# Gated linear attention followed by a maxout feed-forward block: packing transfers issued ahead of loads, output steps moved behind the next group's last unit, weight rounding split in two halves

## The chip, the cores and the metric

One core of a Trainium2 chip runs the whole program. The metric is device time in microseconds of one execution; lower is better. The kernel before and the changed kernel compute the same function on the same inputs.

## The reference

The first block is a linear attention with a gated state, for 4 batches of 8 heads, 768 positions, head size 48. The second is a feed-forward block with three input weights and an elementwise maximum.

```python
f = 1 / (1 + exp(-f_logit))
for t in range(768):                       # per batch and head
    state = f[t][:, None] * state + outer(k[t], v[t])
    y[t]  = q[t] @ state
x = y as (3072 tokens, 384)                # 8 heads side by side
h = maximum(maximum(x @ w1, x @ w2), x @ w3)   # 384 -> 768
out = h @ w_out                            # 768 -> 384
```

The weights arrive as 8-byte words; the kernel rounds them to 4-byte floats itself, with bit operations.

## The kernel before

**Units.** The sequence is cut into chunks of 64 positions. A unit is one chunk of two batches with all heads; there are 24 units, and unit u holds chunk u // 2 of batch pair u % 2. Four units make a group of 512 tokens, so there are 6 groups. For a unit, `sigmoids` and `products` make the gates, their running products (a scan on VectorE, L255), the transposed k and q (through TensorE for units 0 to 7, by VectorE transposes at L232 from unit 8 on) and q times the products; `quotients` makes the reciprocals (L274) and `kh` (GpSimd, L275) in two halves. `keys` transposes `kh` back on TensorE (L288), `pairs` makes the scores (L301) and masks them (L304), `values` multiplies them with v and updates the state (L318 to L335). `finish` adds the part from the state (L348), copies the result from PSUM to `xT` with ScalarE (L357), copies the fourth heads' part to `last` (L354), and **packs** it: six small transfers from `last` into the free rows of `xT` (L362). With them the group's `xT` is a dense 384 x 512 operand.

**Feed-forward block.** `ffn(g, xT)` is a generator of 22 steps: 18 products with a slice of w1, w2 or w3 (L373, 6 TensorE instructions a step) whose results are evacuated by ScalarE (L377) or VectorE (L379), and 4 output steps (L388, 12 TensorE instructions a step), each with a ScalarE copy (L391) and two stores (L395). `fill(n)` runs n steps of it between the parts of the next group's units. Before the next group's `ffn` is made, `fill(99)` empties the old one. Two PSUM tiles take the results of steps in turn.

**Weights.** They come in 15 pieces. `load_weight` (L196) starts a piece's transfer into one of 4 raw buffers. `round_weight` rounds one: VectorE L208, ScalarE L211, GpSimd add L212, VectorE L213, ScalarE L217, VectorE L218, which writes the weight tile; then it starts the load of the piece four further on. Pieces 0 to 2 are rounded after unit 1, pieces 3 to 14 within the steps of group 0, each ahead of its use.

**Order.** The program's order is the order of each engine's instructions; nothing is reordered. Transfers are started by SyncE (SP), one after the other, except k and q of unit 0, which ScalarE starts. A transfer at the head of SP's list that has to wait holds everything behind it. `load(u)` for units up to 7 is 6 transfers (L145) and `load_v` 2; from unit 8 on, `load(u)` of an even unit fetches f, k and q for two units in 24 transfers (L158). In the main loop an even unit u begins with `load(u + 2)` and `load_v(u + 2)`, and only then come `fill`, `keys(u)` and `finish(u - 1, xT)`. In the opening loop over units 0 to 3 `load(u + 4)` and `load_v(u + 4)` follow `values(u)`, ahead of the `finish` of that unit.

Of the kernel before, what the change touches and what calls it, by code (L numbers as in the profile page):

```python
# [9 lines left out]
FP32 = mybir.dt.float32  # L10
I32 = mybir.dt.int32
U32 = mybir.dt.uint32
AF = mybir.ActivationFunctionType
# [31 lines left out]
DP = 64  # L45
# [7 lines left out]
def kernel(  # L53
# [12 lines left out]
    nc = tc.nc  # L66
# [3 lines left out]
    UT = 2 * C  # L70
# [18 lines left out]
    def fast():  # L89
        ctx = ExitStack()  # L90
        with ctx:
# [71 lines left out]
            def load_v(u):  # L163
                load_tokens(v_tiles[u % NLD], v, u)
# [32 lines left out]

            def round_weight(n):
                if n in raw:
                    dst = pieces[n][0]  # L200
                    a, w = dst.shape[1:]
                    N = a * w
                    words = raw.pop(n)[:, 0:2 * N].rearrange("p (n two) -> p n two", two=2)
                    lo, hi = words[:, :, 0], words[:, :, 1]


                    top = work.tile([128, 768], U32, name="top_bits")[:, 0:N]
                    nc.vector.tensor_scalar(top, hi, 3, 0x3FFFFFF8, op0=ALU.logical_shift_left, op1=ALU.bitwise_and)  # L208

                    rest = work.tile([128, 768], U32, name="rest_bits")[:, 0:N]  # L210
                    nc.scalar.activation(rest, lo, AF.Copy, scale=2.0 ** -29)  # L211
                    nc.gpsimd.tensor_tensor(top, top, rest, op=ALU.add)  # L212
                    nc.vector.scalar_tensor_tensor(top, hi, 0xC0000000, top, op0=ALU.bitwise_and, op1=ALU.bitwise_or)  # L213


                    size = work.tile([128, 768], FP32, name="size")[:, 0:N]
                    nc.scalar.activation(size, hi.bitcast(FP32), AF.Square)  # L217
                    nc.vector.scalar_tensor_tensor(dst, size.rearrange("p (a c) -> p a c", a=a), HI_MIN ** 2,  # L218
                                                   top.bitcast(FP32).rearrange("p (a c) -> p a c", a=a),
                                                   op0=ALU.is_ge, op1=ALU.mult)  # L220
                load_weight(n + RAW)

# [116 lines left out]

            def finish(u, xT):  # L340
                d = ready.pop(u)
# [17 lines left out]
                for par in range(2):  # L359
                    for i in range(NK):  # L360
                        p0 = par * DP
                        nc.sync.dma_start(out=xT[p0 + D:p0 + DP, i, t0:t0 + UT],  # L362
                                          in_=last[p0 + i * TAIL:p0 + (i + 1) * TAIL, :])


            def ffn(g, xT):
                hm = work.tile([128, NJ, TOK], FP32, name="hm", bufs=1)
                for j in range(NJ):
                    top = None
                    for i in range(3):  # L370
# [11 lines left out]
                        if g == 0 and (step < 6 or step % 2 == 0):  # L382
                            round_weight(3 + step if step < 6 else 6 + step // 2)
                        yield
# [12 lines left out]

            pending = iter(())

            def fill(n):  # L400
                for _ in range(n):
                    next(pending, None)

# [3 lines left out]


            with tc.manual_schedule():
                for u in range(GRP):  # L410
                    load(u, nc.scalar if u == 0 else nc.sync)
                    load_v(u)
                for n in range(RAW):
# [4 lines left out]
                for u in range(GRP):  # L418
                    keys(u)
                    if u > 1:  # L420
                        finish(u - 1, xT)
                    pairs(u)
                    if u + 2 < GRP:
                        gates(u + 2)
                    values(u)
                    load(u + GRP)
                    load_v(u + GRP)
                    if u == 0:
                        finish(u, xT)
                    if u == 1:  # L430
                        for n in range(3):
                            round_weight(n)

                nc.tensor.transpose(ps_tr.tile([128, 128], FP32, name="tr"), ident, ident)
                finish(GRP - 1, xT)
                pending = ffn(0, xT)
                fill(1)
# [6 lines left out]
                for u in range(GRP, NU):  # L444
                    n = u + 1
                    if BY_ROWS <= u + 2 < NU and u % 2 == 0:
                        load(u + 2)
                    if GRP <= u + 2 < NU and u + 2 >= 2 * GRP:
                        load_v(u + 2)
                    fill(2 if u % 2 and u < NU - GRP else 1)  # L450
                    keys(u)
                    if u > GRP:
                        finish(u - 1, xT)
                    if u % GRP == 0:
                        if u > GRP:
                            fill(99)
                            pending = ffn(u // GRP - 1, xT)
                        xT = new_xT()
                    pairs(u)
                    if n < NU:  # L460
                        sigmoids(n)
# [8 lines left out]
                    if n < NU:  # L470
                        quotients(n, 1)
                        if n in (5, 7):
                            pad_blocks(n // 2 % 2)
                    fill(1)
                fill(1)
                finish(NU - 1, xT)
                fill(99)
                pending = ffn(NU // GRP - 1, xT)
                fill(99)

# [233 lines left out]
```

## Time and profile before

| | us |
|---|---|
| median of 3 runs | 628.8 (626.64 to 629.12) |
| the profiled execution | 628.61 |
| its span in the trace | 626.9 |
| TensorE busy (matmuls) | 484.0 (77% of the span) |
| VectorE busy | 261.3 (42%) |
| ScalarE busy | 127.6 (20%) |
| GpSimd busy | 100.8 (16%) |

The profiled execution took 1.7 us more than its span. Busy time of TensorE includes stretches at the lower of its two clock levels: the granted clock is given as a share of full speed (2.4 GHz), and half is the lower level. The chain that ended last is TensorE for 66% of the span and SP's list of transfers for 12%.

### The profile page before, as it was taken

What the parts mean: (1) busy time and instruction counts of PE and PEld (TensorE: products, weight loads), DVE (VectorE), ACT (ScalarE), POOL (GpSimd) and SP (SyncE); (2) the same over time, 40 slices, a digit from 0 to 9 for tenths busy, and PEclk for the clock granted to TensorE, in tenths of its full rate; (3) what the DMA queues carried; (4) which work ended last, traced back from release to release, by engine and by line L of the source; (5) the groups of instructions that cost most, each with busy time, mean ns of one, the idle gap of its engine ahead of it and who ended that gap; (6) DMA issues with size and microseconds to landing.
All of it is one profiled execution on the core that took longest, in us unless ns stands there. A gap on an engine that the chain in (4) does not pass through costs nothing.

```text
span 626.9 us, 10135 instructions
## 1 busy us (share of the span) xinstructions
PE 484.0 (77%) x4067; PEld 259.5 (41%) x4067; DVE 261.3 (42%) x321; ACT 127.6 (20%) x297; POOL 100.8 (16%) x139
## 2 busy tenths in 40 slices
PE   5830168597991799990999990999981999999995
PEld 3630035154451355560455550455550444554452
DVE  6840055746634256542356532366431466101110
ACT  3431043233221022211022220022220022120000
POOL 4410032444232010110011010011110011000000
PEclk9765597887996799996899995899995999999998
DMA  9756355535026106026015026015035000010001
GB/s 141 167 107 139 66 101 109 126 90 71 4 56 89 29 10 85 18 46 96 16 21 76 17 56 87 14 26 75 13 64 80 13 4 5 17 42 0 0 14 44
DMA packets 166761, 34.99 MB, mean 56 GB/s; under 512 B 155952, under 2 KB 163632, under 8 KB 166704
## 3 DMA queue, kind: packets, MB, share of 16 engines
q1 hardware_dynamic: 164592, 33.85, 31.5%
q10 hardware_dynamic: 2112, 0.39, 0.4%
q8 instruction: 34, 0.56, 0.4%
q14 instruction: 23, 0.19, 0.1%
HBM read 28.31 MB, written 4.72 MB: 53 GB/s over the span
## 4 chain that ended last, share of the span: by engine, by line
PE 66%; SPq 12%; DVE 9%; issue 4%; POOL 3%; DMA 2%; ACT 2%; DVEq 0%; POOLq 0%; ACTq 0%
PE p L373 43%; PE p L388 13%; SPq L158 5%; DVE inv L274 4%; SPq L145 3%; POOL top_bits L212 2%; PE y L348 2%; SPq L362 2%; PE y L318 2%; PE tr L288 2%; PE a L301 2%; DMA xT<-last 1%; PE y L327 1%; DVE top_bits L213 1%; DVE prod L255 1%
## 5 line engine op out<-in xcount | busy, mean ns | idle before, releaser
L373 PE MATMUL p<-xT,w_in 128*128 128x512 f32 x648 | 304.4, 624 | 95.5 <-DMA xT<-last 87.9
L373 PEld LDWEIGHTS p<-xT,w_in 128*128 128x128 f32 x648 | 125.7, 200 | 244.0 <-issue 234.2
L388 PE MATMUL p<-w_out,hm 128*128 128x384 f32 x288 | 95.5, 488 | 1.5 <-DVE hm L379 1.5
L379 DVE TENSOR_TENSOR top<-p,top 128x512 f32<-128x512 f32 x36 | 24.5, 681 | 164.6 <-PE p L373 164.6
L274 DVE RECIPROCAL inv<-prod 128x256 f32<-128x256 f32 x48 | 82.5, 1734 | 0.3
L377 ACT COPY top<-p 128x512 f32<-128x512 f32 x36 | 21.1, 586 | 280.1 <-PE p L373 280.1
L388 PEld LDWEIGHTS p<-w_out,hm 128*128 128x128 f32 x288 | 54.2, 190 | 40.3 <-issue 2.9
L268 POOL TENSOR_TENSOR qh<-qt,prod 128x512 f32<-128x512 f32 x24 | 28.3, 1178 | 206.7 <-DVE qt L232 130.1
L275 POOL TENSOR_TENSOR kh<-kt,inv 128x256 f32<-128x256 f32 x48 | 36.2, 754 | 157.2 <-DVE inv L274 157.2
L379 DVE TENSOR_TENSOR hm<-p,top 128x512 f32<-128x512 f32 x36 | 24.3, 675 | 35.3 <-PE p L373 35.1
L304 DVE TENSOR_TENSOR at<-a,mask 128x512 f32<-128x512 f32 x24 | 16.5, 687 | 51.8 <-PE a L301 51.8
L213 DVE SCALAR_TENSOR_TENSOR top_bits<-raw,top_bits 128x768 uint32<-128x768 uint32 (+1 forms) x15 | 12.0, 800 | 61.2 <-POOL top_bits L212 61.2
L255 DVE TENSOR_TENSOR_SCAN prod<-gate,floor 128x520 f32<-128x520 f32 x24 | 29.7, 1238 | 7.8 <-issue 4.5
L391 ACT COPY o<-p 128x384 f32<-128x384 f32 x24 | 11.5, 479 | 104.7 <-PE p L388 96.6
L212 POOL TENSOR_TENSOR top_bits<-top_bits,rest_bits 128x768 uint32<-128x768 uint32 (+1 forms) x15 | 22.2, 1483 | 62.7 <-ACT rest_bits L211 43.0
L288 PE MATMUL tr<-ident,kh 128*128 128x128 f32 x88 | 16.3, 317 | 17.7 <-POOL kh L275 17.7
L318 PE MATMUL y<-at,v_ld 64*64 64x64 f32 x768 | 18.0, 236 | 9.8 <-issue 8.8
L290 ACT COPY ks<-tr 128x512 f32<-128x512 f32 x22 | 12.9, 585 | 60.2 <-PE tr L288 60.2
L318 PEld LDWEIGHTS y<-at,v_ld 64*64 64x64 f32 x768 | 14.6, 144 | 25.0 <-issue 23.6
L288 PEld LDWEIGHTS tr<-ident,kh 128*128 128x128 f32 x88 | 12.2, 161 | 27.4 <-POOL kh L275 19.9
L357 ACT COPY xT<-y 64x192 f32<-64x192 f32 (+1 forms) x72 | 22.7, 316 | 1.3
L354 ACT COPY last<-y 64x64 f32<-64x64 f32 (+1 forms) x72 | 15.0, 209 | 23.8 <-DMA xT<-last 12.4
(56 smaller groups left out, 275.6 us busy)
## 6 DMA issues: line engine op xcount, KB each, us to landing
v_ld<-in_v_dram SPq DMA_DIRECT2D x48, 96.0 KB, 2.9
out_dram<-o SPq DMA_DIRECT2D x48, 96.0 KB, 2.2
raw<-in_moe_w_dram SPq DMA_DIRECT2D x12, 288.0 KB, 4.8
xT<-last SPq DMA_DIRECT2D x144, 8.0 KB, 1.8
raw<-in_moe_w_out_dram SPq DMA_DIRECT2D x3, 768.0 KB, 4.4
f_ld<-in_f_logit_dram SPq DMA_DIRECT2D x32, 64.0 KB, 2.5
k_ld<-in_k_dram SPq DMA_DIRECT2D x32, 64.0 KB, 2.5
q_ld<-in_q_dram SPq DMA_DIRECT2D x32, 64.0 KB, 2.5
```

The lines of the kernel that those rows point to most:

```text
L158: nc.sync.dma_start(out=blocks[nm][u // 2 % 2][p0:p0 + 32, n, :, 0:w], in_=src[:, par::2, t0 + n * 32:t0 + (n + 1) * 32, e0:e0 + w].rearrange(
L212: nc.gpsimd.tensor_tensor(top, top, rest, op=ALU.add)
L255: nc.vector.tensor_tensor_scan(scan.rearrange("p x t -> p (x t)"), gate.rearrange("p x t -> p (x t)"), floor.rearrange("p x t -> p (x t)") ...
L268: nc.gpsimd.tensor_tensor(qh, qt, prod, op=ALU.mult)
L274: nc.vector.reciprocal(d["inv"][:, a], d["prod"][:, a])
L275: nc.gpsimd.tensor_tensor(d["kh"][:, :, a, :], d["kt"][:, a], d["inv"][:, a], op=ALU.mult)
L288: nc.tensor.transpose(tr_s[:, hp, :], kh[:, hp].rearrange("p a t -> p (a t)"), ident)
L318: nc.tensor.matmul(y[o:o + DP, a, hp * C:(hp + 1) * C], lhsT=v_ld[s, 2 * hp + par, :], rhs=d["at"][s, par, hp, :], start=(hp == 0), stop=F ...
L357: nc.scalar.copy(xT[o, :, t0 + a * C:t0 + (a + 1) * C], y[i, a, 0:NK * C].rearrange("p (h t) -> p h t", h=NK))
L373: nc.tensor.matmul(p, lhsT=w_in[i][:, kt, j * 128:(j + 1) * 128], rhs=xT[:, kt, :], start=(kt == 0), stop=(kt == NK - 1))
L379: nc.vector.tensor_tensor(hm[:, j, :] if i == 2 else top, p, top, op=ALU.max)
L388: nc.tensor.matmul(p[:, 0:DM], lhsT=hm[:, j, i * UT:(i + 1) * UT], rhs=w_out[:, j, :], start=(j == 0), stop=(j == NJ - 1))
```

## The change

1. In the main loop `load(u + 2)` and `load_v(u + 2)` move from the head of unit u to behind `pairs(u)`, that is, behind the packing of unit u - 1.
2. `pending` becomes a list of generators. A group's `ffn` is appended instead of being started after `fill(99)`, so the rest of the old one runs first. From unit 4 to 8 one `fill(1)` less per unit is done, from then on 22 steps per group as before. At the border of two groups (u = 8, 12, 16, 20) one output step stands before `keys(u)` and two stand between `pairs(u)` and `values(u)`.
3. In the opening, the packing of units 0 to 2 is started by ScalarE, that of unit 3 half by SP and half by ScalarE. `load` and `load_v` of unit u + 4 stand behind the `finish` or the rounding of unit u, those of unit 7 behind the packing of unit 3. v of two units is loaded after f, k and q of both.
4. `round_weight(n)` becomes `round_begin(n)` (L208, L211, L212, L217) and `round_end(n)` (L213, L218, next load). A step that needed `round_weight(n)` runs `round_end(n)` and then `round_begin(n + 1)`. Pieces 0 to 2 are begun after unit 1 and ended after unit 2's `values`. `top_bits` and `size` get three buffers.

```diff
+            def round_begin(n):
                 if n in raw:
...
                     nc.vector.tensor_scalar(top, hi, 3, 0x3FFFFFF8, op0=ALU.logical_shift_left, op1=ALU.bitwise_and)
...
                     nc.scalar.activation(rest, lo, AF.Copy, scale=2.0 ** -29)
                     nc.gpsimd.tensor_tensor(top, top, rest, op=ALU.add)
+                    size = work.tile([128, 768], FP32, name="size", bufs=3)[:, 0:N]
+                    nc.scalar.activation(size, hi.bitcast(FP32), AF.Square)
+                    halfway[n] = (top, hi, size)
+
+            def round_end(n):
+                if n in raw:
...
+                    top, hi, size = halfway.pop(n)
                     nc.vector.scalar_tensor_tensor(top, hi, 0xC0000000, top, op0=ALU.bitwise_and, op1=ALU.bitwise_or)
...
+                    del raw[n]
                 load_weight(n + RAW)
...
-            def finish(u, xT):
+            def finish(u, xT, queues=(nc.sync, nc.sync)):
...
-                        nc.sync.dma_start(out=xT[p0 + D:p0 + DP, i, t0:t0 + UT],
+                        queues[par].dma_start(out=xT[p0 + D:p0 + DP, i, t0:t0 + UT],
...
-                            round_weight(3 + step if step < 6 else 6 + step // 2)
+                            n = 3 + step if step < 6 else 6 + step // 2
+                            round_end(n)
+                            round_begin(n + 1)
...
-            pending = iter(())
+            pending = []
...
-                for _ in range(n):
-                    next(pending, None)
+                while n and pending:
+                    try:
+                        next(pending[0])
+                        n -= 1
+                    except StopIteration:
+                        pending.pop(0)
...
-                    load_v(u)
+                    if u % 2:
+                        load_v(u - 1)
+                        load_v(u)
...
-                        finish(u - 1, xT)
+                        finish(u - 1, xT, (nc.scalar, nc.scalar))
...
-                    load(u + GRP)
-                    load_v(u + GRP)
                     if u == 0:
-                        finish(u, xT)
+                        finish(u, xT, (nc.scalar, nc.scalar))
                     if u == 1:
                         for n in range(3):
-                            round_weight(n)
+                            round_begin(n)
+                    if u == 2:
+                        for n in range(3):
+                            round_end(n)
+                        round_begin(3)
+                    if u < GRP - 1:
+                        load(u + GRP)
+                        load_v(u + GRP)
...
-                finish(GRP - 1, xT)
-                pending = ffn(0, xT)
+                finish(GRP - 1, xT, (nc.sync, nc.scalar))
+                load(2 * GRP - 1)
+                load_v(2 * GRP - 1)
+                pending.append(ffn(0, xT))
...
                 for u in range(GRP, NU):
                     n = u + 1
-                    if BY_ROWS <= u + 2 < NU and u % 2 == 0:
-                        load(u + 2)
-                    if GRP <= u + 2 < NU and u + 2 >= 2 * GRP:
-                        load_v(u + 2)
-                    fill(2 if u % 2 and u < NU - GRP else 1)
+                    fill(2 if u % 2 and u > 2 * GRP else 1)
                     keys(u)
                     if u > GRP:
                         finish(u - 1, xT)
                     if u % GRP == 0:
                         if u > GRP:
-                            fill(99)
-                            pending = ffn(u // GRP - 1, xT)
+                            pending.append(ffn(u // GRP - 1, xT))
                         xT = new_xT()
                     pairs(u)
+                    if BY_ROWS <= u + 2 < NU:
+                        if u % 2 == 0:
+                            load(u + 2)
+                        load_v(u + 2)
...
-                    fill(1)
+                    if u >= 2 * GRP:
+                        fill(1)
                 fill(1)
                 finish(NU - 1, xT)
-                fill(99)
-                pending = ffn(NU // GRP - 1, xT)
+                pending.append(ffn(NU // GRP - 1, xT))
                 fill(99)
```

## Rows read from the trace of the kernel before

**Rows 1.** The page's DMA issues: transfers, KB each, median us from issue to landing.

```profile
xT<-last SPq DMA_DIRECT2D x144, 8.0 KB, 1.8
...
q_ld<-in_q_dram SPq DMA_DIRECT2D x32, 64.0 KB, 2.5
```

**Rows 2.** Waits of TensorE, whole span: total us, times, longest.

```profile
PE p L373 <- DMA xT<-last: 87.9, 5, 26.9
PE tr L288 <- POOL kh L275: 17.7, 4, 6.1
```

**Rows 3.** Timeline at a border of two groups: start us, length us, instructions.

```profile
279.71 4.37 SPq L158 DMA_DIRECT2D f_ld<-in_f_logit_dram  x8
...
282.21 0.66 PE L348 MATMUL y<-qh,st 48*48 48x64 f32 x32
...
288.42 4.15 SPq L158 DMA_DIRECT2D q_ld<-in_q_dram  x8
...
295.54 3.73 SPq L362 DMA_DIRECT2D xT<-last  x6
...
299.31 7.70 PE L373 MATMUL p<-xT,w_in 128*128 128x512 f32 x12 [15.97 <-DMA xT<-last]
```

**Rows 4.** Timeline at the last border, where no loads are left.

```profile
548.92 0.66 PE L348 MATMUL y<-qh,st 48*48 48x64 f32 x32
...
549.51 8.01 PE L388 MATMUL p<-w_out,hm 128*128 128x384 f32 x24
...
551.03 4.46 SPq L362 DMA_DIRECT2D xT<-last  x6
...
557.36 3.17 PE L373 MATMUL p<-xT,w_in 128*128 128x512 f32 x7
```

**Rows 5.** Stretches: length, busy us by engine, granted clock, DMA share, GB/s.

```profile
75.40:207.40 132.00, 93.37 (x769) 50.80 (x769) 69.11 (x82) 39.47 (x77) 42.32 (x46) 0.82 0.42 78
...
282.90:299.30 16.40, 0.44 (x32) 0.32 (x23) 3.84 (x5) 2.21 (x8) 1.31 (x2) 0.62 0.62 88
...
484.30:557.50 73.20, 73.20 (x577) 37.08 (x578) 29.12 (x35) 13.09 (x36) 7.32 (x10) 0.97 0.06 14
557.50:619.40 61.90, 61.90 (x159) 29.39 (x157) 8.30 (x12) 5.43 (x10) 0.00 (x0) 1.00 0.06 14
```

**Rows 6.** The chain that ended last, in order of time: start us, us, what.

```profile
228.05 5.35 PE p L373 x12
...
392.53 7.17 PE p L373 x12
```

**Rows 7.** SP's list of transfers in the opening, timeline of SP alone.

```profile
44.97 6.92 SPq L196 DMA_DIRECT2D raw<-in_moe_w_dram  x12
...
66.05 1.34 SPq L145 DMA_DIRECT2D f_ld<-in_f_logit_dram  x2
...
70.20 1.29 SPq L145 DMA_DIRECT2D v_ld<-in_v_dram  x2
71.58 3.74 SPq L362 DMA_DIRECT2D xT<-last  x6
```

**Rows 8.** Timeline of the first 20 us, three of its rows.

```profile
0.82 1.41 ACTq L145 DMA_DIRECT2D k_ld<-in_k_dram  x2
...
12.22 1.18 DVE L255 TENSOR_TENSOR_SCAN prod<-gate,floor 128x520 f32<-128x520 f32 x1
...
12.38 1.54 POOL L275 TENSOR_TENSOR kh<-kt,inv 128x256 f32<-128x256 f32 x1 [0.73 <-DVE inv L274]
```

**Rows 9.** Waits in group 0's stretch (75.4 to 207.4 us).

```profile
DVE top_bits L213 <- POOL top_bits L212: 57.7, 12, 33.6
...
PE p L373 <- DMA xT<-last: 38.6, 2, 26.9
```

**Rows 10.** Groups of instructions in the same stretch.

```profile
L212 POOL TENSOR_TENSOR top_bits<-top_bits,rest_bits 128x768 uint32<-128x768 uint32 x9 | 16.3, 1808 | 15.3 <-DVE top_bits L208 15.1
...
L275 POOL TENSOR_TENSOR kh<-kt,inv 128x256 f32<-128x256 f32 x10 | 7.8, 775 | 29.2 <-DVE inv L274 29.2
```

More of the change, by code (lines that the diff above doesn't have):

```diff
@@ L196, in load_weight @@
                     nc.sync.dma_start(out=d, in_=s)
-            def round_weight(n):
+            halfway = {}
+            def round_begin(n):
                 if n in raw:
-                    dst = pieces[n][0]
-                    a, w = dst.shape[1:]
+                    a, w = pieces[n][0].shape[1:]
                     N = a * w
-                    words = raw.pop(n)[:, 0:2 * N].rearrange("p (n two) -> p n two", two=2)
+                    words = raw[n][:, 0:2 * N].rearrange("p (n two) -> p n two", two=2)
                     lo, hi = words[:, :, 0], words[:, :, 1]
-                    top = work.tile([128, 768], U32, name="top_bits")[:, 0:N]
+                    top = work.tile([128, 768], U32, name="top_bits", bufs=3)[:, 0:N]
                     nc.vector.tensor_scalar(top, hi, 3, 0x3FFFFFF8, op0=ALU.logical_shift_left, op1=ALU.bitwise_and)
@@ L212, in round_weight @@
                     nc.gpsimd.tensor_tensor(top, top, rest, op=ALU.add)
+                    size = work.tile([128, 768], FP32, name="size", bufs=3)[:, 0:N]
[3 more added lines that the diff above has]
+                if n in raw:
+                    dst = pieces[n][0]
+                    a = dst.shape[1]
+                    top, hi, size = halfway.pop(n)
                     nc.vector.scalar_tensor_tensor(top, hi, 0xC0000000, top, op0=ALU.bitwise_and, op1=ALU.bitwise_or)
-                    size = work.tile([128, 768], FP32, name="size")[:, 0:N]
-                    nc.scalar.activation(size, hi.bitcast(FP32), AF.Square)
                     nc.vector.scalar_tensor_tensor(dst, size.rearrange("p (a c) -> p a c", a=a), HI_MIN ** 2,
```

## Prediction, made before the changed kernel was run

> **What bounds the kernel now.** I read the page first. TensorE is busy 77% of the span and no other engine over 42%, so either TensorE's own work or its waits set the time. Its part on transfers shows that they are short: a packing transfer lands 1.8 us after issue, a block of q 2.5 [rows 1]. The list of TensorE's waits says what is long: the input products (L373) stand 87.9 us before a packing transfer lands, in 5 waits, the longest 26.9 us; the next, for `kh`, is 17.7 us over 4 [rows 2]. 38.6 of the 87.9 fall into the stretch of group 0, as two waits [rows 9], so one is 26.9 us, ahead of the first feed-forward product at 75.4 us, one is 11.7 at the border to group 1, and the three later borders share 87.9 - 38.6 = 49.3.
>
> The timeline at a border shows why [rows 3]. The last thing the packing needs, the state part of unit 11's result, leaves TensorE at 282.87. SP has by then begun the loads of units 14 and 15: f starts at 279.71, q ends at 292.57, 24 transfers in 12.9 us. Only then, at 295.54, come the six packing transfers, and the first product at 299.31. The stretch holds 16.4 us with 0.4 of matmuls [rows 5]. The transfers are not slow; they are started late.
>
> The last border is the counter-example, because no loads are left there [rows 4]: the state part ends at 549.58, packing starts at 551.03 and its last start ends at 555.49, and TensorE meanwhile runs two output steps, 8.0 us. The product follows at 557.36 without a wait. That is the changed kernel's border in small.
>
> After a wait there is a second cost. Twelve product instructions take 7.17 us behind one [rows 6] and 7.70 behind another [rows 3], but 5.35 in the middle of a group [rows 6]; the granted clock in the stalled stretch is 0.62, and 0.97 to 1.00 in the last two busy stretches [rows 5]. So each border pays 1.8 to 2.3 us more for a restart at half clock, about 2.1.
>
> **Later borders (edits 1 and 2).** The loads leave the place ahead of the packing; two of the old group's output steps stand behind it as cover. No instruction is added. Ready time after the state part: 555.49 - 549.58 = 5.9 us to the last start, and a transfer lands 1.8 us after issue [rows 1], so at most 7.7 for the last of six; the first is needed earliest. Cover: 8.0 us of output steps, and `pairs` and `values` besides. What stands ahead of the packing on SP's list is then two v transfers long past and the stores of the output step before `keys`, whose copy ends before the state part does. So I cost the wait at nothing; without the two output steps it would be some 6 us a border. Gain: 49.3 of waits, and four half-clock restarts (the border to group 1 too) at 2.1, 8.4: **-57.7**. What is late next is the load itself, which now follows `pairs`; it is a rival below.
>
> **Opening (edit 3).** SP's list is the clock there: 12 weight transfers end at 51.89, then packs and loads alternate up to 75.32, and the first product starts at 75.40 [rows 7]. Off the list go: unit 7's load, from 66.05 to 71.49, 5.4 us; three packs of 3.7 to 3.9, 11.3; half a pack, 1.9. Sum 18.6, so 56.8. What is new: the loads of weight pieces 4 to 6 wait for raw buffers that are now freed only after unit 2's `values`, and SP holds unit 6's load and the last pack behind them. Before, the list was late enough for this not to show. No row shows the new wait; I take 2 us, near the lower end of nothing to 8, because the bit operations of the first half no longer hold VectorE up ahead of unit 2. The 18 packing starts move to ScalarE: two starts took it 1.41 us [rows 8], so a pack 4.2 us, in which its evacuations of the following unit wait. Nothing if SP's list still ends last, 8.4 if two packs stand on the path: that is the upper end. First product at 58.8 instead of 75.4: **-16.6** (55 to 67).
>
> The Trainium skill speaks against this part: DMA: Bandwidth & Descriptors, section "Issuing engines are not separate DMA queues", says that starting transfers on several engines saves only the issuer's time, usually small beside the transfer. Here the rows show issue times as the whole delay (3.74 us for six starts); by the page's rule the moved packs would give nothing, and the start would come at 70.0.
>
> **Group 0 (edits 2 and 4).** It takes 132.0 us with 93.4 of matmuls [rows 5], so 38.6 idle: 11.7 at its border, which goes as above, and 26.9 elsewhere, mostly for `kh`. There VectorE is the tight engine: 69.1 us busy, and its second half of a rounding waits for GpSimd's add, 57.7 us in 12 waits, 33.6 of them one wait for the opening [rows 9]. So 24.1 us of VectorE standing still with reciprocals, masks and evacuations behind it, in order. The split removes these: the add of piece n + 1 now runs under the steps between. It adds nothing but two buffers.
>
> How much of it TensorE gets back is the unclear term. I walked through the new order, instruction by instruction with these durations: nearly all of the rounding still falls into the 18 product steps, VectorE is close to full there, and `keys` of units 5 to 8 still find `kh` late, because GpSimd's add stands ahead of it (1.81 us) and the reciprocal behind a rounding half. I find four to five waits of 3 to 5 us, 19 in all: 26.9 - 19 = 8 gained. Against that, overlap has a price. Once a scan at 12.22 took 1.18 us and `kh`, started at 12.38, 1.54 [rows 8] instead of its mean 0.775 [rows 10]: GpSimd lost 0.8 us beside a two-operand VectorE instruction. The new order puts the adds (1.808 each [rows 10]) right ahead of four scans; if each holds a scan up in full, 7 us; I take 3. Sum: -11.7 - 8 + 3 = **-16.7**. Bounds: all 26.9 come back (-38.6), or none and the full 7 is paid (-4.7).
>
> The skill's SBUF — State Buffer, section "SBUF: two separate sides", gives the pair of ports that VectorE and GpSimd share as an exclusive lock for a whole instruction. The row agrees in direction; by the rule every collision is paid in full.
>
> **Sum.** 626.9 - 57.7 - 16.6 - 16.7 = 535.9 of span. The profiled execution took 628.61, 1.7 more than its span and level with the median of 628.8, so the time is 537.6: I say **537**. The floor is far off: six groups of 61.9 [rows 5] are 371, and units, opening and tail take the rest.
>
> **The rivals.**
>
> *Rounding stays the bound of group 0.* Adds and VectorE's two-operand instructions exclude each other, and in place of waiting for the add VectorE waits for the port. For it: the lengthened `kh`. Against: reciprocals, the longest VectorE work, have one operand. Group 0 then keeps 127 us and the time is 537 + 12 = 549.
>
> *The moved packs give nothing*, since ScalarE's own delay (4.2 us each) puts unit 3 as late as SP did, or because only issue time is saved. By the page on issuing engines it would be so. For it: the three packs stand in the busiest part of ScalarE's opening. First product at 70.0, time 549.
>
> *The packing is still late at the borders.* It would do so if something else on SP's list waits, a store of an output step for its copy, for instance. Against: the last border has just these stores and no wait [rows 4]. If half of the 49.3 and of the restarts stay, 566.
>
> *Group 0 frees fully.* Its 26.9 go nearly all: 537 - 19 = 518.
>
> *Slower: the loads are late.* Place: VectorE's transposes of k and q for unit u + 2, in unit u + 1, with evacuations queued behind them and two PSUM tiles of slack. After the state part, packing takes SP until 5.9, 24 starts 12.9, landing 2.5 [rows 1]: 21.3 us. They are needed after two output steps 8.0, four product steps at 2.7 each and about one unit's own TensorE work, (73.2 - 61.9) / 4 = 2.8: 21.5 us, and q some 2 us after that. So the margin is thin but positive; a late load costs its lateness beyond one step. There are 8 such loads, so the kernel gets slower only when each holds TensorE over 94 / 8 = 11.8 us: 631 at 12 us.
>
> **How the numbers follow.** The forecast 0.56 (its own range 524 to 546), rounding as bound 0.17, packs give nothing 0.07, packing late 0.07, group 0 free 0.11, late loads 0.02. With ends of unknown terms the range is 516 to 560; beyond it lie the late packing, the late loads and a little of the free group, under 0.2. A measurement of this kernel tells from no change about 0.5%, the spread of the three runs being 0.4%. Faster 0.97, same 0.01, slower 0.02.
>
> **What would show it.** Borders: TensorE's waits for packing vanish or fall under 2 us each, the packing transfers start about 1.5 us after the state part, and 12 product instructions behind them take 5.3 us. Opening: first product between 55 and 67. Group 0: from there to group 1's first product 115 us, VectorE's wait for the add near nothing, `kh` still the longest wait. Wrong would be: a new wait of VectorE's transposes for loads, ScalarE idle or late in the opening, or scans much over 1.2 us beside the adds.

## The result, and the profile after

The changed kernel took **553.2 us** (median of 4 runs, 549.1 to 553.4) beside 629.0 for the kernel before (4 runs): a ratio of 0.878, interval 0.873 to 0.883. The forecast was 537, range 516 to 560. So the direction and the range held, and the likeliest value was 16 us low. The profiled execution took 553.05 us, its span is 551.3; it is 75.6 shorter than the 626.9 of before.

The page of the changed kernel (busy us, share of the span, instructions; then one group of part 5). Line numbers have moved: the products are now L382, packing L371, rounding L209 to L226, reciprocals L283, `kh` L284, `keys` L297, state part L357, output steps L399.

```profile
PE 475.6 (86%) x4067; PEld 256.5 (47%) x4067; DVE 263.7 (48%) x321; ACT 127.2 (23%) x297; POOL 102.2 (19%) x139
...
L382 PE MATMUL p<-xT,w_in 128*128 128x512 f32 x648 | 296.0, 609 | 23.7 <-DMA xT<-last 21.0
```

No engine does much less: TensorE is busy 476 us where it was busy 484, and its share rose to 86% because its waits went. TensorE's waits over the whole span (total us, times, longest), which answer to [rows 2]:

```profile
PE tr L297 <- POOL kh L284: 22.2, 5, 8.9
PE p L382 <- DMA xT<-last: 21.0, 1, 21.0
...
PE p L382 <- ACT top L386: 2.7, 4, 0.7
```

The 87.9 us of waits for a packing transfer in 5 places have become 21.0 us in one, the opening. The four borders have none left. `kh` now takes the most in total, 22.2 us in 5 waits. The stretches, which answer to [rows 5] (length; then busy us of PE, PEld, DVE, ACT, POOL; granted clock; DMA share; GB/s):

```profile
0.00:72.07 72.07, 27.34 (x513) 22.76 (x514) 33.44 (x50) 20.52 (x49) 17.93 (x36) 0.69 0.70 124
72.07:187.26 115.19, 94.11 (x833) 52.14 (x833) 70.02 (x79) 38.55 (x75) 42.79 (x45) 0.85 0.42 83
187.26:261.92 74.66, 73.98 (x686) 38.97 (x685) 40.95 (x48) 16.44 (x42) 11.39 (x16) 1.00 0.37 57
```

Cut at the first product of group 0 and that of group 1, the account against the prediction is:

| part of the span | before | after | gain | predicted |
|---|---|---|---|---|
| opening, to group 0's first product | 75.40 | 72.07 | 3.3 | 16.6 |
| group 0, to group 1's first product | 132.00 | 115.19 | 16.8 | 16.7 |
| the rest | 419.5 | 364.0 | 55.5 | 57.7 |
| span | 626.9 | 551.3 | 75.6 | 91.0 |

Almost the whole miss, 13.3 of 15.4 us, is the opening. Group 0 agrees to a tenth, which the experiments show to be luck of two errors. A border in the timeline (start us, length us, what; it answers to [rows 3]):

```profile
251.77 0.66 PE L357 MATMUL y<-qh,st 48*48 48x64 f32 x32
...
252.83 8.01 PE L399 MATMUL p<-w_out,hm 128*128 128x384 f32 x24
...
253.89 3.73 SPq L371 DMA_DIRECT2D xT<-last  x6
...
257.67 4.29 SPq L158 DMA_DIRECT2D f_ld<-in_f_logit_dram  x8
...
261.85 10.57 PE L382 MATMUL p<-xT,w_in 128*128 128x512 f32 x24
...
267.34 4.15 SPq L158 DMA_DIRECT2D q_ld<-in_q_dram  x8
...
279.91 0.67 DVE L241 STREAM_TRANSPOSE qt<-q_ld 128x512 f32<-128x512 f32 x1
```

Packing starts 1.5 us after the state part ends and is issued before the loads; two output steps run meanwhile; 24 product instructions take 10.57 us, that is 5.3 for 12, where 12 took 7.70 in [rows 3]; and the granted clock over the whole group that follows, group 1, is 1.00 (the row 187.26:261.92), the upper level. The loads come later than before but in time: q's last start ends at 271.49, plus the 2.5 us to landing [rows 1] is 274.0, and its transpose begins at 279.91. The margin is 6 us, where the prediction had some 2.

The opening is the surprise. SP's own list, which answers to [rows 7]:

```profile
36.88 1.85 SPq L145 DMA_DIRECT2D f_ld<-in_f_logit_dram  x2
41.41 1.73 SPq L145 DMA_DIRECT2D k_ld<-in_k_dram  x2
...
44.88 1.29 SPq L145 DMA_DIRECT2D v_ld<-in_v_dram  x2
49.06 1.48 SPq L145 DMA_DIRECT2D f_ld<-in_f_logit_dram  x2
...
55.90 6.28 SPq L196 DMA_DIRECT2D raw<-in_moe_w_dram  x12
62.22 1.28 SPq L145 DMA_DIRECT2D f_ld<-in_f_logit_dram  x2
...
68.93 1.87 SPq L371 DMA_DIRECT2D xT<-last  x3
```

The list has holes: SP stands from 38.73 to 41.41 and from 46.17 to 49.06, in front of loads that need no data of a pack. SP's waits between 18 and 72 us name what it stood for, and ScalarE's starts in the timeline agree: in either hole SP goes on 1.7 and 2.4 us after ScalarE begins a pack.

```profile
SPq L145 <- DMA xT<-last: 10.3, 4, 3.9
```

```profile
39.68 4.07 ACTq L371 DMA_DIRECT2D xT<-last  x6
...
46.68 4.46 ACTq L371 DMA_DIRECT2D xT<-last  x6
```

SP waits 10.3 us for packing transfers, though ScalarE starts those. The experiments below follow this up, and then take group 0 and the borders apart.

### The profile page after: what moved, and what is told of

Same layout as the page of the kernel before. It is cut to its first block, busy times and chain, and to the rows that moved or that the text cites. A ratio compares the mean times of both kernels' runs of the same rounds, so it can differ in the third digit from the quotient of the medians.

```text
span 551.3 us, 10105 instructions
## 1 busy us (share of the span) xinstructions
PE 475.6 (86%) x4067; PEld 256.5 (47%) x4067; DVE 263.7 (48%) x321; ACT 127.2 (23%) x297; POOL 102.2 (19%) x139
## 4 chain that ended last, share of the span: by engine, by line
PE 76%; DVE 6%; SPq 4%; DMA 3%; issue 3%; ACT 2%; POOL 2%; ACTq 2%; DVEq 0%; POOLq 0%
PE p L382 48%; PE p L399 17%; DVE inv L283 2%; PE y L357 2%; SPq L145 2%; PE y L327 2%; PE a L310 2%; PE tr L297 2%; SPq L196 2%; ACTq L371 2%; PE y L336 1%; DMA raw<-in_moe_w_dram 1%; POOL top_bits L213 1%; PE tr L237 1%; DMA xT<-last 1%
## 5 line engine op out<-in xcount | busy, mean ns | idle before, releaser
L382 PE MATMUL p<-xT,w_in 128*128 128x512 f32 x648 | 296.0, 609 | 23.7 <-DMA xT<-last 21.0
L382 PEld LDWEIGHTS p<-xT,w_in 128*128 128x128 f32 x648 | 122.4, 194 | 167.0 <-issue 157.6
L399 PE MATMUL p<-w_out,hm 128*128 128x384 f32 x288 | 95.3, 488 | 0.0
L283 DVE RECIPROCAL inv<-prod 128x256 f32<-128x256 f32 x48 | 82.0, 1730 | 0.3
L399 PEld LDWEIGHTS p<-w_out,hm 128*128 128x128 f32 x288 | 54.2, 190 | 38.0 <-issue 2.4
L386 ACT COPY top<-p 128x512 f32<-128x512 f32 x36 | 21.1, 585 | 191.9 <-PE p L382 191.9
L284 POOL TENSOR_TENSOR kh<-kt,inv 128x256 f32<-128x256 f32 x48 | 36.1, 753 | 77.0 <-DVE inv L283 77.0
L264 DVE TENSOR_TENSOR_SCAN prod<-gate,floor 128x520 f32<-128x520 f32 x24 | 29.7, 1238 | 29.2 <-ACT gate L253 24.0
L213 POOL TENSOR_TENSOR top_bits<-top_bits,rest_bits 128x768 uint32<-128x768 uint32 (+1 forms) x15 | 23.8, 1588 | 76.2 <-ACT rest_bits L212 38.5
L297 PE MATMUL tr<-ident,kh 128*128 128x128 f32 x88 | 16.4, 318 | 22.3 <-POOL kh L284 22.2
L297 PEld LDWEIGHTS tr<-ident,kh 128*128 128x128 f32 x88 | 12.0, 161 | 32.9 <-POOL kh L284 26.4
L327 PEld LDWEIGHTS y<-at,v_ld 64*64 64x64 f32 x768 | 14.7, 145 | 23.2 <-issue 13.1
L343 DVE TENSOR_TENSOR st<-y,st 128x384 f32<-128x384 f32 x20 | 11.1, 553 | 23.9 <-PE y L336 23.9
L363 ACT COPY last<-y 64x64 f32<-64x64 f32 (+1 forms) x72 | 15.0, 208 | 21.1 <-PE y L357 16.8
```

Of the source, the lines that this page charges most:

```text
L264: nc.vector.tensor_tensor_scan(scan.rearrange("p x t -> p (x t)"), gate.rearrange("p x t -> p (x t)"), floor.rearrange("p x t -> p (x t)") ...
L283: nc.vector.reciprocal(d["inv"][:, a], d["prod"][:, a])
L284: nc.gpsimd.tensor_tensor(d["kh"][:, :, a, :], d["kt"][:, a], d["inv"][:, a], op=ALU.mult)
L297: nc.tensor.transpose(tr_s[:, hp, :], kh[:, hp].rearrange("p a t -> p (a t)"), ident)
L327: nc.tensor.matmul(y[o:o + DP, a, hp * C:(hp + 1) * C], lhsT=v_ld[s, 2 * hp + par, :], rhs=d["at"][s, par, hp, :], start=(hp == 0), stop=F ...
L382: nc.tensor.matmul(p, lhsT=w_in[i][:, kt, j * 128:(j + 1) * 128], rhs=xT[:, kt, :], start=(kt == 0), stop=(kt == NK - 1))
```

## The experiments

"First product" is always the first feed-forward product, "group 0" the stretch from it to group 1's first product. All times are of the profiled execution where a stretch is named, medians otherwise.

### The opening: what holds the packing of unit 3

**All packs back on SP.** If ScalarE's starts had freed SP of 13 us, taking them back must cost that.

```diff
-                        finish(u - 1, xT, (nc.scalar, nc.scalar))
+                        finish(u - 1, xT)
...
-                        finish(u, xT, (nc.scalar, nc.scalar))
+                        finish(u, xT)
...
-                finish(GRP - 1, xT, (nc.sync, nc.scalar))
+                finish(GRP - 1, xT)
```

> The changed kernel with one thing undone: all packing transfers of the opening are started by SP again. Theory A: in the changed kernel SP's transfers wait for packs that ScalarE starts late, because transfers of both issuers take eight completion semaphores in turn, and a transfer waits until the one eight places ahead of it has landed. Then putting 21 starts back on SP costs nothing: first feed-forward product at 68 to 72 us (75.4 of the kernel before, less unit 7's load, 5.4), total 549 to 554. Theory B: SP's list is simply full, and the moved starts did save their 13 us: first product near 85 us, total near 566.

Measured 551.2 us (ratio to the kernel before 0.876, 0.873 to 0.879), first product at 71.82. The 21 starts on ScalarE are worth nothing at all: SP with all four packs is as early as SP without three and a half of them.

**The same, with the loads of units 5 to 7 moved behind it.**

```diff
-                    if u < GRP - 1:
+                    if u == 0:
                         load(u + GRP)
                         load_v(u + GRP)
...
-                load(2 * GRP - 1)
-                load_v(2 * GRP - 1)
+                load(GRP + 1)
+                load_v(GRP + 1)
...
                     pairs(u)
+                    if u + 2 < BY_ROWS:
+                        load(u + 2)
+                        load_v(u + 2)
```

> As the previous kernel, and besides units 5 to 7 are loaded later: unit 5 behind the packing of unit 3, units 6 and 7 within units 4 and 5. Theory A: SP's list now ends with the packs as soon as their data are there; first product at 55 to 59 us, group 0 as long as in the changed kernel (115 us), total 536 to 541. Theory B: the list is full; two loads less are 11 us, first product near 74. Rival to the gain: the later loads hold the gates of units 5 to 7, first product at 57 and group 0 at 120 or more.

Measured 540.0 us (0.859, 0.856 to 0.861), first product at 60.03, 1 us later than expected. So the order on SP's list decides, as the prediction said; what it had wrong is which entries had left the list.

**No packs of units 0 to 2.** Their rows of `xT` stay at zero, so the output of group 0 is not the block's. In the place of each pack ScalarE makes copies of about the same length; unit 3's pack stays half on SP, half on ScalarE. If ScalarE's own starts delayed the opening, nothing changes; if SP waited for those transfers, the first product comes at once at the predicted place.

```diff
+                if queues is None:
+                    for _ in range(6):
+                        nc.scalar.copy(spare, floor.rearrange("p x t -> p (x t)")[:, 0:512])
-                for par in range(2):
+                for par in range(2 if queues else 0):
...
-                        finish(u - 1, xT, (nc.scalar, nc.scalar))
+                        finish(u - 1, xT, None)
...
-                        finish(u, xT, (nc.scalar, nc.scalar))
+                        finish(u, xT, None)
```

> The changed kernel with the packing transfers of units 0 to 2 left out (their rows of xT are zeros) and, in each one's place, a ScalarE copy of about the same length, so that ScalarE is as busy as before. Theory A: SP's transfers wait for those of ScalarE through the completion semaphores that both share. Without them SP's list runs through, and the first product comes at 57 to 60 us as the prediction's count had it (58.8). Rival: ScalarE's time or the raw buffers hold the opening; then the first product stays at 68 to 72.

One run: 550.1 us, first product at 70.03 (here packing is L374 and the products are L385). Taken by the total, or by the first product, the theory of the semaphores failed. But SP's part of the timeline shows a different opening (with ScalarE's three starts of unit 3 between):

```profile
39.95 1.29 SPq L145 DMA_DIRECT2D v_ld<-in_v_dram  x2
...
52.54 1.90 ACTq L374 DMA_DIRECT2D xT<-last  x3
...
54.45 5.91 SPq L196 DMA_DIRECT2D raw<-in_moe_w_dram  x12
```

From 29.6 us on SP now ran without a hole to 41.24, and then stood 13.2 us in front of a weight load, until ScalarE had started its three transfers of unit 3. Its waits say the same:

```profile
SPq L196 <- DMA xT<-last: 13.1, 1, 13.1
```

A weight load needs nothing of `xT`. Its raw buffer was free at 43.5 us, when VectorE's L223 for the first piece ended, so that some 11 of the 13.2 us have another cause. The compiled program's list of instructions (engine, line, what, and the semaphores that it waits for) tells which:

```
SP   L145 DMA k_ld0_104<-in_k_dram 64x8x48 [waits DMAHW2_49]
ACT  L374 DMA xT_186<-last_702 16x128 [waits DMAHW3_49,Activation_49]
SP   L145 DMA k_ld0_104<-in_k_dram 64x8x48 [waits DMAHW4_49]
ACT  L374 DMA xT_186<-last_702 16x128 [waits DMAHW5_49]
ACT  L374 DMA xT_186<-last_702 16x128 [waits DMAHW6_49]
SP   L145 DMA q_ld0_106<-in_q_dram 64x8x48 [waits DMAHW7_49]
...
SP   L196 DMA raw_560<-in_moe_w2_dram 48x3x256 [waits DMAHW3_49,DVE_49,Activation_49]
```

The rows of the two engines are put in one list here by the number of the semaphore. There are eight, DMAHW0 to 7, and transfers take them in turn, those of SP and of ScalarE out of the same eight; a transfer waits until the one before it on its semaphore has landed. ScalarE's three hold numbers 3, 5 and 6, and SP's next transfer on number 3 is the weight load. So a transfer that ScalarE can start only late holds SP's list, eight transfers further on, just as if it stood in that list.

**The same without ScalarE's last three starts**: unit 3's pack all on SP, the others still left out. If the semaphores are it, this alone brings the prediction's first product.

```diff
-                finish(GRP - 1, xT, (nc.sync, nc.scalar))
+                finish(GRP - 1, xT)
```

> The kernel without the packs of units 0 to 2 (zeros in their rows of xT, ScalarE copies in their place), with unit 3's pack started by SP alone, so that in the opening ScalarE starts no transfer but unit 0's k and q. In the run before, SP stood from 41 to 54 us, and its wait ended with the three transfers of unit 3 that ScalarE starts. Theory A (completion semaphores shared by both issuers, taken in turn): that wait goes, first product at 57 to 60 us, total 536 to 541. Rival (raw buffers or ScalarE's time): first product stays at 68 to 72.

One run: 538.1 us, first product at 59.97. The timeline of SP, TensorE's first product, and SP's longest wait up to 59 us:

```profile
39.43 1.29 SPq L145 DMA_DIRECT2D v_ld<-in_v_dram  x2
42.84 5.99 SPq L196 DMA_DIRECT2D raw<-in_moe_w_dram  x12
...
56.18 3.77 SPq L374 DMA_DIRECT2D xT<-last  x6
...
59.97 4.35 PE L385 MATMUL p<-xT,w_in 128*128 128x512 f32 x6 [9.53 <-DMA xT<-last]
...
SPq L196 <- DVE top_bits L223: 2.1, 1, 2.1
```

SP waits 2.1 us for the raw buffers and nothing else of size; the three more starts cost 1.9 us on its list and the first product came 10.1 us earlier. That settles the cause: without ScalarE's early packs SP's four waits of the changed kernel are gone, and without its last three starts the one that was left is gone too.

### Group 0: what the split and the borders are worth there

**Rounding whole again, all else as changed.** `round_begin` and `round_end` run one behind the other, at the places that they had before.

```diff
+                            round_begin(n)
                             round_end(n)
-                            round_begin(n + 1)
...
-                        round_begin(3)
```

> The changed kernel with the rounding of pieces 3 to 14 whole again: both halves in one step. The prediction's step: VectorE waits some 24 us for GpSimd's adds again, TensorE sees about 8 of it, less 3 us of port collisions: group 0 at 120 us instead of 115, total 556 to 560. Rival: the split gives nothing, group 0 within 2 us of 115. Second rival: VectorE's waits are all on TensorE's path, group 0 at 130 or more.

Measured 570.5 us (0.908, 0.906 to 0.911). Group 0 took 131.1 us, 16 more than with the split, against 5 by the prediction's terms; the total is 10 us over the one expected. The wait for `kh` there, whole rounding first (TensorE's waits in 71.72 to 202.86 us):

```profile
PE tr L297 <- POOL kh L284: 34.1, 5, 12.3
```

and with the split (72.1 to 187.2 us of the changed kernel):

```profile
PE tr L297 <- POOL kh L284: 19.9, 4, 8.9
```

**The border edits alone, on the kernel before** (edits 1 and 2 without 3 and 4), and **the split alone** (edit 4's rounding in two halves within the steps of group 0, nothing else). Their diffs are the lines of those edits shown above.

> The kernel before with the borders' edits alone (loads behind the packing, output steps behind the border); opening and rounding as before. Additive: first product at 75.4, the later groups as in the changed kernel, group 0 at 131 as with whole rounding, total 569 to 574. By the prediction's terms (borders -57.7, group 0's border -11.7): total 557 to 561.

> The kernel before with the rounding of pieces 3 to 14 split and nothing else. If the split has a worth of its own in group 0 (16 us in the changed kernel): total 611 to 616. By the prediction's term (8 back, 3 paid): 622 to 625. If it pays only together with the later place of the feed-forward steps: within 3 us of the 628 of before.

Border edits alone: 575.3 us (0.914, 0.912 to 0.916). From group 1's first product on it takes 364.3 us, as the changed kernel does (364.0), so the later borders' gain is that of these edits. Group 0 took 132.7 us where the kernel before takes 132.0. The wait of 11.7 us at its border is gone, and nothing of it is earned: TensorE's waits for `kh` in this stretch (75.4 to 207.4 us before, 76.1 to 208.8 here) grew from the first of these lines to the second:

```profile
PE tr L288 <- POOL kh L275: 16.6, 3, 6.1
...
PE tr L288 <- POOL kh L275: 33.7, 4, 12.3
```

The likely reason, which no run isolates: with fewer steps per unit the rounding, which sits in the steps, is spread beside more units' reciprocals; the run without cover below, which puts the steps back, speaks for it. The split alone: 616.2 us (0.980, 0.978 to 0.982), group 0 at 117.4 us, 14.6 less.

**Reciprocals one step earlier**, on the version with packs on SP and loads later. The edit moves those of units 5 to 8, which are made during units 4 to 7.

```diff
                         products(n)
+                        if u < 2 * GRP:
+                            quotients(n, 0)
                     fill(1)
                     values(u)
                     if n < NU:
-                        quotients(n, 0)
+                        quotients(n, 1 if u < 2 * GRP else 0)
                     fill(1)
                     if n < NU:
-                        quotients(n, 1)
+                        if u >= 2 * GRP:
+                            quotients(n, 1)
```

> The kernel of 540 us (packs on SP, later loads) with the reciprocals of units 6 to 8 made one feed-forward step earlier, ahead of two roundings instead of between them. If VectorE's order makes kh late, TensorE's waits for kh fall from 22 to about 10 us, total 528 to 533. Rival: VectorE is full, and the time comes back as waits for evacuations, total 538 to 542.

Measured 526.8 us (0.837, 0.836 to 0.839), 1 us under the range expected; group 0 took 101.4 us, 12.8 less than the 114.2 of the version that it was built on, and the waits for `kh` over the whole span fell from 22.5 us in 5 to

```profile
PE tr L297 <- POOL kh L284: 11.9, 3, 5.5
```

TensorE's idle time in group 0 fell from 21.1 us to 11.3, and its busy time from 93.1 to 90.1 with the granted clock at 0.91 in place of 0.87. So nearly half of the idle time that was left hung on the place of the reciprocals behind a rounding half on VectorE's list, and not on the amount of VectorE's work, which is the same.

### The borders: cover and loads

**No output steps behind the group.** `fill(99)` empties the old group before the new one is appended, so packing has no output steps to hide behind.

```diff
-                    fill(2 if u % 2 and u > 2 * GRP else 1)
+                    fill(2 if u % 2 and u < NU - GRP else 1)
...
                         if u > GRP:
+                            fill(99)
                             pending.append(ffn(u // GRP - 1, xT))
...
-                    if u >= 2 * GRP:
-                        fill(1)
+                    fill(1)
```

> The changed kernel with the old feed-forward generator emptied at each border and the old number of steps per unit: the loads stay behind the packing, but no output step covers it. The prediction's step: a wait of about 5 us plus 2 us of restart at each of four borders, total 575 to 582. Rival: pairs and values hide the packing anyway, total within 3 us of the changed kernel's 553.

Measured 571.2 us (0.908, 0.906 to 0.911). TensorE's waits, whole span:

```profile
PE p L382 <- DMA xT<-last: 39.7, 5, 20.4
```

Without the opening's 20.4 that is 19.3 us over four borders, 4.8 each, beside the prediction's "some 6" for this wait. From group 1's first product to the end the kernel takes 385.7 us in place of 364.0: three of the waits, 14.8 us, and four restarts at the lower clock. The fourth wait, 4.5 us, lies in group 0, which became 3.3 us shorter all the same (111.9), and so the total stayed below the expectation: group 0's steps stand at their old places again, and its waits for `kh` fell from 19.9 us in 4 to 10.6 in 3.

**The loads of f, k and q one unit later**, the slower rival made to happen.

```diff
                     if BY_ROWS <= u + 2 < NU:
-                        if u % 2 == 0:
-                            load(u + 2)
                         load_v(u + 2)
+                    if BY_ROWS <= u + 1 < NU and u % 2:
+                        load(u + 1)
```

> The changed kernel with the loads for two units moved one unit later still, to the odd unit just ahead of their use. The prediction's slower rival, enforced: f, k and q land some 17 us behind the need at eight places; beyond two PSUM tiles of slack TensorE stands 8 to 14 us at each: total 615 to 665. If loads are hidden however late (fewer than 3 us each): under 580.

One run: 652.2 us, slower than the kernel before. ScalarE's gates now wait for the loads (a gate reads f alone; the view names the `k_ld` transfers that land at about the same time),

```profile
ACT sig L256 <- DMA k_ld<-in_k_dram: 71.9, 7, 10.7
```

and TensorE behind them, whose waits for ScalarE's evacuation of a product grew from 2.7 us in 4 to

```profile
PE p L382 <- ACT top L386: 32.6, 7, 6.7
```

The span is 98.9 longer than that of the changed kernel, 12.4 for each of the 8 loads. So the rival's mechanism is real, and its price per load is what the prediction had put as the point where the kernel loses; the changed kernel has 6 us of margin before such a load is late at all.

### A version that beats both

**Weight pieces 5 and 6 loaded behind unit 3's pack, and unit 4's reciprocals one step earlier too**, on top of the version with earlier reciprocals.

```diff
-                load_weight(n + RAW)
+                if n not in (1, 2):
+                    load_weight(n + RAW)
...
                 finish(GRP - 1, xT)
+                load_weight(1 + RAW)
+                load_weight(2 + RAW)
...
                 products(GRP)
-                fill(1)
                 quotients(GRP, 0)
                 fill(1)
                 quotients(GRP, 1)
+                fill(1)
```

> The kernel of 526.8 us, with the loads of weight pieces 5 and 6 put behind the packing of unit 3 and the reciprocals of unit 5's gates one step earlier. If the packs wait for the landing of the weight pieces ahead of them: first product at 53 to 56 instead of 59.9, total 520 to 524. Rival: pieces 5 and 6 then come late to their rounding, and the time goes back there, total 526 to 530.

The reciprocals that move are those of unit 4, as the diff shows. Measured **518.0 us** (517.7 to 519.8; ratio 0.825, 0.822 to 0.829), 2 us under the range expected. First product at 54.88, 5.0 earlier than in the version that it was built on; group 0 in 96.9 us, 4.5 less; the rest 364.2, as in the changed kernel. TensorE is busy 467.0 us, 91% of the span. The two edits were not run apart.

## Why the prediction was partly right

**Opening: the step that failed.** "Off the list go: unit 7's load ... three packs ... half a pack ... Sum 18.6, so 56.8." The sum itself was right: 58.8 was forecast with 2 us for the raw buffers, and where ScalarE starts no pack the first product came at 59.97 with 2.1 us for them, though there SP starts all six transfers of unit 3, 1.9 us more than the sum has. What was wrong is that a transfer which another engine starts is off SP's list. The first product came at 72.07, gain 3.3 in place of 16.6: SP waited for ScalarE's packs through the shared semaphores, 10.3 us in 4 waits. The bounds of 55 to 67 did not hold it either; their upper end reckoned with ScalarE's delay and not with a wait of SP.

**The rival "the moved packs give nothing"** had this outcome (70.0 and 549 forecast, 72.07 and 553 measured), at a chance of 0.07, by another way than the two that it named. ScalarE's starts did take what the prediction had from [rows 8]: 3.96 to 4.46 us for six. The Trainium skill, DMA: Bandwidth & Descriptors, section "Issuing engines are not separate DMA queues", says that starts on several engines save the issuer's time alone. Here they saved not even that: packs on SP or on ScalarE gave 71.82 and 72.07. The prediction's "by the page's rule the moved packs would give nothing" took the page further than it goes, since the issuer's time was just what the sum reckoned with.

**Group 0: the right sum of wrong terms.** Forecast -11.7 for the border, -8 for the split, +3 for collisions; measured -16.8. Alone, the border edits gave +0.7 and the split -14.6. The wait at the border did go, but the waits for `kh` grew by 17.1 us and took back what the border had gained; that the steps moved into later units did this is likely, and not isolated. The split was worth 14.6 us alone and 16 on top of the other edits, where the prediction had 8: VectorE's wait for the add, which it was to remove, fell from 24.1 us to 1.4. The walk through the order had the number and the sum of the remaining waits right, four to five and 19 in all against 19.9 us in 4, though one of them is 8.9 and not 3 to 5; it was set against the wrong start, since of the 26.9 us only 16.6 were waits for `kh` before, and the border edits raised these to some 34.

**Collisions: right size, other place.** No scan was lengthened (1236 ns mean before, 1238 after). Three other instructions were, the most of all (mean ns behind the comma; two lines of before, 75.4 to 207.4 us, then three of after, 72.0 to 187.2 us):

```profile
L213 DVE SCALAR_TENSOR_TENSOR top_bits<-raw,top_bits 128x768 uint32<-128x768 uint32 x9 | 8.6, 960 | 21.8 <-POOL top_bits L212 21.8
...
L335 DVE TENSOR_TENSOR st<-st,prod 128x384 f32<-128x384 f32 x4 | 2.8, 703 | 0.1
...
L213 POOL TENSOR_TENSOR top_bits<-top_bits,rest_bits 128x768 uint32<-128x768 uint32 x9 | 17.9, 1984 | 35.0 <-DVE top_bits L209 24.4 <-ACT rest_bits L212 9.0 <-ACT size L215 1.6
L223 DVE SCALAR_TENSOR_TENSOR top_bits<-raw,top_bits 128x768 uint32<-128x768 uint32 x9 | 10.3, 1146 | 1.4 <-POOL top_bits L213 1.4
...
L344 DVE TENSOR_TENSOR st<-st,prod 128x384 f32<-128x384 f32 x4 | 4.2, 1046 | 0.1
```

Before, the add took 1808 [rows 10], and the two on VectorE 960 and 703: 9 times 0.19 and 4 times 0.34 are 3.1 us on VectorE, about the 3 that the prediction took. The timeline shows who pays:

```profile
100.53 1.23 DVE L264 TENSOR_TENSOR_SCAN prod<-gate,floor 128x520 f32<-128x520 f32 x1
100.75 2.61 POOL L213 TENSOR_TENSOR top_bits<-top_bits,rest_bits 128x768 uint32<-128x768 uint32 x1 [5.92 <-DVE top_bits L209]
...
103.32 1.17 POOL L277 TENSOR_TENSOR qh<-qt,prod 128x512 f32<-128x512 f32 x1
103.39 1.91 DVE L223 SCALAR_TENSOR_TENSOR top_bits<-raw,top_bits 128x768 uint32<-128x768 uint32 x1 [1.06 <-POOL top_bits L213]
...
106.99 1.80 POOL L213 TENSOR_TENSOR top_bits<-top_bits,rest_bits 128x768 uint32<-128x768 uint32 x1 [1.63 <-ACT size L215]
107.34 1.86 DVE L344 TENSOR_TENSOR st<-st,prod 128x384 f32<-128x384 f32 x1
```

In each of the three pairs the one that began first takes its usual time and the other one is longer, by 0.80, 0.95 and 1.16 us. The scan began first, so the add paid for it, where the prediction let the scan pay. That the later one waits agrees with the exclusive lock that the prediction cited from the Trainium skill's SBUF — State Buffer, section "SBUF: two separate sides". The two of each pair overlap by 1.01, 1.10 and 1.45 us, so the later one lost some four fifths of the overlap and not quite all of it.

**Later borders: right.** -57.7 forecast, -55.5 measured. The residue is about that of four waits of 0.7 us for ScalarE's copy of a product (L386), 2.7 us together, one in each of groups 1 to 4, the first ahead of the product at 209.13 us; why they came, no run shows. Waits, start of packing, time of the first 12 products and granted clock came as listed. The rival "packing late" is out, and that of late loads was shown to be real one unit further on; here the margin was on the safe side, 6 us where the prediction had some 2.

**Rounding as bound** (549) had a time near the measured one, but not its reason: group 0 did not keep 127 us, and the collisions cost VectorE some 3 us. A total near a rival's does not speak for the rival.

## What to carry to other kernels

Before a transfer is moved to another engine, ask what else it shares with those that stay: here eight completion semaphores, taken in turn, chained SP's loads to packs that ScalarE could start only late, and the engine change gave nothing where moving loads behind the packs on SP's own list gave 11 us. Price an edit in a stretch where one in-order engine is close to full by what the next stage needs from that engine and when: the same work in another order on VectorE was worth 12.8 us, and a wait that is removed at one place came back whole at another. Two edits whose terms add up to the measured sum can both be mis-sized, so measure each alone.

## What the runs showed of the hardware and the program that was not expected

- Transfers of SP and ScalarE wait for each other through eight semaphores that the compiled program hands out in turn: 13.1 us in one wait of SP, of which 2.1 stayed, for a raw buffer, when ScalarE's three starts went. Whether ScalarE's starts would pay with semaphores of their own was not tried.
- In the three pairs shown, of a two-input instruction of VectorE and one of GpSimd, it was the later one that grew, on either engine: a rounding half to 1.91 us (0.96 before), a state update to 1.86 (0.70), an add to 2.61 behind a scan (1.81).
